# One decode step of attention and MLP: w2's first half loaded ahead of V, masked exponentials, and wo's rows 0 to 15 in one load

## The chip, the cores and the metric

The kernel runs on one core of a Trainium2 chip. The metric is the device time of one execution in microseconds (us), taken as the median of several runs. Beside the timed runs there is one profiled execution, whose records carry times from the start of its span. The engines are PE (matrix multiply, with PEld for its weight loads), DVE (vector), ACT (activations), POOL and SP; SP only issues loads here. Sixteen DMA engines move the data.

## The reference

One token x (1024 values) goes through an outer layernorm, then through attention and an MLP side by side, and everything is added to x:

```python
xn = _layernorm(x, axis=-1)
return x + _A_ref(xn, A_k_cache, A_v_cache, A_wq, A_wo) + _B_ref(xn, B_w1, B_b1, B_w2, B_b2)

# _A_ref: 32 query heads, 4 key/value heads, head size 128, the last W = 4096 positions of the caches
q = (x @ wq).reshape(B, Sq, Hq, Dh).transpose(0, 2, 1, 3)
k = jnp.repeat(k_cache[:, :, Sk - W:, :], rep, axis=1)   # rep = 8 query heads share one k/v head
v = jnp.repeat(v_cache[:, :, Sk - W:, :], rep, axis=1)
p = _softmax(jnp.einsum("bhqd,bhkd->bhqk", q, k) * (Dh ** -0.5))
o = jnp.einsum("bhqk,bhkd->bhqd", p, v)
return o.transpose(0, 2, 1, 3).reshape(B, Sq, Hq * Dh) @ wo

# _B_ref: y = _layernorm(x); h = gelu(y @ w1 + b1), 3584 values; return h @ w2 + b2
```

All weights are bf16: wq is 1024 x 4096, wo 4096 x 1024, w1 1024 x 3584, w2 3584 x 1024. With one token, every weight is used once, so the kernel has to bring some 40 MB on the chip for very little arithmetic.

## The kernel before

The program is a list of steps, each with its engine, the names that it reads and the names that it writes. `Plan` turns these names into semaphore waits; on each engine the steps run in the order in which they are written. All large loads are issued by SP, in one queue, in this order: a first row of wq (8 KB for each of the 128 partitions), K (4 MB), the rest of wq in loads of one, two and four rows, b1 and b2, w1 in two halves, V (4 MB), w2's rows 0 to 5, 6 to 13 and 14 to 27, wo's rows 0 to 7 and 8 to 15, and wo's rows 16 to 31 cut at 8, 12, 14 and 15. "Row" here means one row of the `(p c) n` view: row c of w2 is 1024 values for each of the 128 partitions.

Four buffers of 32 KB for each partition, `slot[0]` to `slot[3]`, hold all of this in turn, so a load also waits until the buffer's last reader is done. Slot 0 holds K, then w1's second half, then wo's rows 0 to 15. Slot 1 holds wq's first half, w1's first half and w2's rows 14 to 27. Slot 2 holds wq's second half, V, and wo's rows 16 to 31. Slot 3 holds K transposed in blocks (`kt_scr`), then w2's rows 0 to 13.

The work is in these stages:

- x is spread over the partitions by four small matmuls (`x_ps`, `spread`), normalised on DVE, and laid into `xw`.
- K is transposed in 32 x 32 blocks by DVE (L341) and regrouped into `kT` by ACT (L346) and DVE (L350), while PE multiplies xw by wq (L376, in a loop).
- Scores: q is transposed and laid into `qm`, a 128 x 32 weight block for each key/value head with only that head's eight columns filled; 32 matmuls of 512 columns give the scores in `sc_ps`. Their maximum goes over the partitions through PE, and ACT takes the exponential (L457) into `e128`, with the sums in `l_loc`.
- w1: eight rows, each in four column tiles of PE, in two parts, `w1_part(0)` before and `w1_part(1)` behind the maximum. DVE adds b1 (`h_pre`, L471), ACT takes gelu, DVE transposes it into `hT` and copies it into `hTf`.
- V: the exponentials are transposed in blocks into `eTb` (L461), and 32 matmuls of 512 columns (`v_step`, L502) multiply blocks of 128 columns of eTb by one position of all four heads. Each partition holds 32 positions of each head. The 32 rows of the result hold every query head against every key/value head; `gmask`, scaled by the reciprocal of the sums (`grs`), picks each head's own on DVE (`o_m`, `o_f`, `o_bf`).
- w2: DVE multiplies 21 of its 28 rows by hTf and adds them up in two accumulators, `run[0]` and `run[1]` (L489): nine rows before it looks at V's result, twelve behind. PE does the other seven, `PE_ROWS`.
- wo: o is spread over the partitions (`o8`), and PE multiplies its 32 rows. Rows 0 to 15 go one at a time, 16 to 23 in pairs on two column tiles, all into `sc_ps`; DVE adds these to run[0] (L557), the result is added by PE to rows 24 to 31 (`acc_a`, `acc_b`), DVE and ACT cast it, and two small loads store it.

Of the kernel before, what the change touches and what calls it, by code (L numbers as in the profile page):

```python
# [142 lines left out]
def kernel(  # L143
# [27 lines left out]
    NJQ = NQ // 512  # L171
    WQ4 = W // 4
# [21 lines left out]
    misc = ps("misc", [P, 512])  # L194
    qo_ps = ps("qo_ps", [P, 512])
# [20 lines left out]
    def op(eng, fn, r=(), w=()):  # L216
        plan.add(eng, fn, r, w)

    def dma(eng, out_ap, in_ap, r=(), w=(), over=()):
        q = plan.engines[eng]  # L220
        plan.add(eng, lambda: q.dma_start(out=out_ap, in_=in_ap), r, w, True, over)  # L221
# [18 lines left out]
    def mm32(out_ap, w_ap, x_ap, start, stop, r, w, pos=None):  # L240
        op("pe", lambda: pe.matmul(out_ap, lhsT=w_ap, rhs=x_ap, start=start, stop=stop, tile_position=pos), r, w)  # L241
# [10 lines left out]
    for i, a, b in wq_cuts:  # L252
# [6 lines left out]

    spread = sb("spread", [Hq, 4, P], BF16)  # L260
# [20 lines left out]

    x_ps, tot = misc[:, 0:C], misc[:, 16:17]
# [4 lines left out]
    op("dve", lambda: dve.tensor_copy(out=xf, in_=x_ps), ("misc",), ("xf",))  # L287
# [32 lines left out]
    op("dve", lambda: dve.tensor_reduce(out=sel4, in_=ident_f.rearrange("p (r h) -> p h r", r=4), axis=AX.X, op=ALU.add), ("ident_f",), ("sel4",))  # L320
    qm = sb("qm", [P, Hkv, Hq], BF16)
# [11 lines left out]
                                          compare_op=ALU.is_equal, fill=0.0, base=0, pattern=[[-1, Hq], [0, Hq]], channel_multiplier=1), ("xb32",), ("run0",))  # L333

# [45 lines left out]
    qz, zrow = qm.rearrange("p g h -> p (g h)")[0:Hq, :], spread.rearrange("p u n -> p (u n)")  # L380
# [40 lines left out]
    qm_d = qm.rearrange("p g h -> p (g h)")  # L421
    qm_d = bass.AP(tensor=qm_d.tensor, offset=qm_d.offset, ap=[list(qm_d.ap[0]), [Hq + REP, Hkv], [1, REP]])
    op("dve", lambda: dve.tensor_copy(out=qm_d, in_=qT_ps.rearrange("p k g -> p g k")), ("qo",), ("qm",))  # L423
    for g in range(Hkv):
        for R in range(4):
            ldw(qm[:, g, :], (0, 32 * R), ("qm",))
        for a in range(2):
            for R in range(4):
                kv = kT[:, R, :, :].rearrange("p u (b r h) -> p h b u r", r=8, h=Hkv)[:, g, 16 * a:16 * a + 16]
                mm(sc_ps[32 * R:32 * R + 32, a, :].rearrange("p (b r u) -> p b u r", r=8, u=4), qm[:, g, :], kv,  # L430
                   g == 0, g == Hkv - 1, (0, 32 * R), kt_keys, (f"sc{a}",))
# [4 lines left out]
    w2_t = [slot[i][:, :14 * D].rearrange("p (r n) -> p r n", r=14) for i in (3, 1)]  # L436
    for a, b in ((0, 6), (6, 14)):
        dma("sp", w2_t[0][:, a:b, :], w2_v[:, a:b, :], (), (f"w20{a}",), kt_srcs)
# [6 lines left out]
    m_row = sb("m_row", [1, Hq], FP32)  # L445
    op("dve", lambda: dve.tensor_reduce(out=m_row, in_=mT_ps.rearrange("a (r h) -> a h r", r=4), axis=AX.X, op=ALU.max), ("misc",), ("m_row",))
    m_rep = sb("m_rep", [1, 4, Hq], FP32)
    op("dve", lambda: dve.tensor_copy(out=m_rep, in_=m_row.unsqueeze(1).to_broadcast([1, 4, Hq])), ("m_row",), ("m_rep",))
    mc_ps = misc[:, 128:129]
    mm32(mc_ps, m_rep.rearrange("a r h -> a (r h)"), ones_f[0:1, 0:1], True, True, ("m_rep", "ones_f"), ("misc",))  # L450
# [8 lines left out]
    eTb = sb("eTb", [P, WQ4 + 96], BF16)  # L459
    op("pool", lambda: pool.memset(eTb[:, WQ4:], 0.0), (), ("eTb_pad",))  # L460
    op("dve", lambda: dve.transpose(out=eTb[:, :WQ4], in_=e128), ("e128",), ("eTb",))  # L461
# [4 lines left out]
    grs = sb("grs", [Hq, Hkv], FP32)  # L466
    op("dve", lambda: dve.tensor_scalar_mul(out=grs, in0=gmask, scalar1=rs), ("gmask", "rs"), ("grs",))


    h_pre = sb("h_pre", [P, 2, NH], FP32)  # L470
    op("dve", lambda: dve.tensor_tensor(out=h_pre, in0=acc2[:, :, :NH], in1=b1x.rearrange("p (b n) -> p b n", b=2), op=ALU.add), ("acc2", "b1x"), ("h_pre",))  # L471
    h_sb = sb("h_sb", [P, 2 * NH], BF16)
    op("act", lambda: act.activation(out=h_sb, in_=h_pre.rearrange("p b n -> p (b n)"), func=ACT.Gelu_apprx_tanh), ("h_pre",), ("h_sb",))
    hT = sb("hT", [P, CW2, 32], BF16)
# [18 lines left out]
    for c in dve_rows[:9]:  # L493
        running(c)


    o_all = qo_ps[0:Hq, :]
    v_in = ("eTb", "eTb_pad", "v0", "slot2")

    def v_step(c, first, last):  # L500
        cols = eTb[:, bass.ds(32 * c, P)] if not isinstance(c, int) else eTb[:, 32 * c:32 * c + P]
        return pe.matmul(qo_ps, lhsT=cols, rhs=v4[:, :, c, :], start=first, stop=last)  # L502
# [14 lines left out]
    o_m = sb("o_m", [Hq, Hkv, Dh], FP32)  # L517
    op("dve", lambda: dve.tensor_tensor(out=o_m, in0=o_all.rearrange("h (g d) -> h g d", g=Hkv), in1=grs.unsqueeze(2).to_broadcast([Hq, Hkv, Dh]), op=ALU.mult), ("qo", "grs"), ("o_m",))
    o_f = sb("o_f", [Hq, Dh], FP32)
    op("dve", lambda: dve.tensor_reduce(out=o_f, in_=o_m.rearrange("h g d -> h d g"), axis=AX.X, op=ALU.add), ("o_m",), ("o_f",))  # L520
    o_bf = sb("o_bf", [Hq, Dh], BF16)
    op("dve", lambda: dve.tensor_copy(out=o_bf, in_=o_f), ("o_f",), ("o_bf",))
    for c in dve_rows[9:]:
        running(c)
# [15 lines left out]
    hcol = lambda c: hT[:, c, 0:1]  # L540
    o8_ps = misc[:, 160:192]
# [71 lines left out]
```

## Time and profile before

| what | us |
|---|---|
| median of 3 timed runs (lowest, highest) | 99.94 (99.74, 100.01) |
| profiled execution | 99.68 |
| its span | 98.4 |
| DMA: share of 16 engines, bytes | 95.7%, 39.86 MB |
| DVE busy | 73.1 |
| PE busy | 56.0 |
| ACT busy | 30.8 |
| POOL busy | 9.9 |

A line of the timeline has the start, the length, the engine and line, what is written and read, the shape, how many instructions were merged, and, in brackets, the idle time before it and what ended that. A line of the chain of waits in order of time has the start, the length and what the time was spent on. The line of a DMA queue has packets, MB and the time its packets took as a share of 16 engines.

### The profile page before, as it was taken

How to read it: one execution, taken by the hardware profiler on the slowest of the kernel's cores; microseconds unless marked ns; L12 is line 12 of the kernel's file. 1: busy time of each engine (PE TensorE's matmuls, PEld its weight loads, DVE VectorE, ACT ScalarE, POOL GpSimd, SP SyncE). 2: the span in 40 equal slices, each digit the busy share in tenths (PEclk: the TensorE clock that was granted, in tenths of full speed). 3: DMA queues.
4: the chain of work that ended last, by engine and by line, in shares of the span. 5: the costliest groups of instructions: out<-in, count | busy, mean ns of one | idle time of the engine just before them, and what ended most of it. 6: DMA issues, size and time to landing. Idle time of an engine off the chain costs nothing.

```text
span 98.4 us, 951 instructions
## 1 busy us (share of the span) xinstructions
PE 56.0 (57%) x323; PEld 16.0 (16%) x220; DVE 73.1 (74%) x75; ACT 30.8 (31%) x29; POOL 9.9 (10%) x22
## 2 busy tenths in 40 slices
PE   0140400699200699930899547977771839595792
PEld 0040000133000234300212211211210101111130
DVE  0146407999999999999005595999989999999231
ACT  0600000099999899992002193000000000000001
POOL 0626810000000670000000000000000000000000
PEclk9999999999996559999579998599999999999999
DMA  3999979999999899989799999999898999999980
GB/s 60 487 426 453 440 310 470 433 533 426 440 426 403 373 385 513 408 373 513 330 426 426 423 438 430 425 426 480 385 524 343 433 426 433 426 433 406 396 323 1
DMA packets 3084, 39.86 MB, mean 405 GB/s; under 512 B 390, under 2 KB 396, under 8 KB 780
## 3 DMA queue, kind: packets, MB, share of 16 engines
q1 hardware_dynamic: 3034, 39.86, 95.7%
q10 hardware_dynamic: 50, 0.00, 0.0%
HBM read 39.86 MB, written 0.00 MB: 405 GB/s over the span
## 4 chain that ended last, share of the span: by engine, by line
DMA 67%; PE 22%; issue 4%; SPq 2%; DVE 0%
DMA slot<-in_A_wq_dram 29%; DMA slot<-in_A_wo_dram 21%; DMA slot<-in_A_v_cache_dram 17%; PE qo_ps L502 12%; PE acc L376 9%; SPq L221 2%; PE acc L241 1%; DVE res L576 0%; PE acc L235 0%
## 5 line engine op out<-in xcount | busy, mean ns | idle before, releaser
L346 ACT COPY kT<-slot 32x1024 bf16<-32x1024 bf16 (+1 forms) x18 | 23.9, 1327 | 15.9 <-DVE slot L341 15.7
L489 DVE SCALAR_TENSOR_TENSOR run<-slot,hTf,run 128x1024 f32<-128x1024 bf16 x20 | 24.2, 1272 | 0.1
L376 PE MATMUL acc<-slot,xw 128*128 x48 | 15.4, 495 | 13.7 <-DMA slot<-in_A_wq_dram 13.7
L341 DVE STREAM_TRANSPOSE slot<-slot 128x4096 bf16<-128x4096 bf16 x4 | 17.4, 4414 | 3.6 <-DMA slot<-in_A_k_cache_dram 3.6
L502 PE MATMUL qo_ps<-slot,eTb 128*128 (+1 forms) x32 | 11.6, 437 | 4.3 <-issue 2.6
L350 DVE COPY kT<-slot 32x4096 bf16<-32x4096 bf16 x10 | 13.2, 1320 | 0.2
L235 PE MATMUL sc_ps<-slot,o 128*1 128x512 bf16 x48 | 9.1, 378 | 4.3 <-DMA slot<-in_A_wo_dram 4.3
L376 PEld LDWEIGHTS acc<-slot,xw 128*128 x48 | 5.5, 115 | 24.3 <-issue 21.9
L577 ACT CAST res<-acc 33x224 bf16<-33x224 f32 x1 | 0.3, 339 | 20.5 <-PE acc L235 20.5
L235 PE MATMUL sc_ps<-kT,qm 128*32 128x512 bf16 x32 | 5.3, 853 | 0.3 <-DVE qm L423 0.3
L502 PEld LDWEIGHTS qo_ps<-slot,eTb 128*128 (+1 forms) x32 | 3.1, 97 | 12.5 <-issue 9.8
L545 ACT CAST o<-misc 128x32 bf16<-128x32 f32 x1 | 0.2, 186 | 15.0 <-PE misc L241 15.0
L227 PEld LDWEIGHTS <-o 128*1 128x1 bf16 x40 | 2.4, 83 | 13.9 <-issue 13.3
L435 DVE COPY sc<-sc_ps 128x512 f32<-128x512 f32 x1 | 0.7, 691 | 4.9 <-PE sc_ps L235 4.9
L241 PE MATMUL acc<-spread,qm 32*128 32x512 bf16 x4 | 1.6, 498 | 3.7 <-POOL qm L322 3.7
L235 PE MATMUL sc_ps<-slot,hT 128*1 128x512 bf16 x14 | 3.2, 378 | 0.5 <-DMA slot<-in_B_w_dram 0.5
L235 PE MATMUL acc<-slot,yT 128*1 128x448 bf16 x64 | 3.4, 353 | 0.0
L434 ACT COPY sc<-sc_ps 128x512 f32<-128x512 f32 x1 | 0.6, 585 | 8.0 <-PE sc_ps L235 8.0
L241 PE MATMUL qo_ps<-selq,q_sb 128*128 128x4 bf16 x8 | 0.4, 166 | 4.3 <-DVE q_sb L395 4.3
L241 PE MATMUL misc<-x,spread 32*128 32x8 bf16 x4 | 0.3, 168 | 4.4 <-POOL spread L262 4.4
L557 DVE TENSOR_TENSOR run<-sc_ps,run 33x512 f32<-33x512 f32 x2 | 1.3, 678 | 1.8 <-PE sc_ps L235 1.8
L235 PE MATMUL acc<-slot,o 128*1 128x288 bf16 (+1 forms) x32 | 2.2, 272 | 0.7 <-DMA slot<-in_A_wo_dram 0.6
(88 smaller groups left out, 43.6 us busy)
## 6 DMA issues: line engine op xcount, KB each, us to landing
slot<-in_B_w_dram SPq DMA_DIRECT2D x3, 3584.0 KB, 16.7
slot<-in_A_wo_dram SPq DMA_DIRECT2D x3, 2048.0 KB, 23.7
slot<-in_A_k_cache_dram SPq DMA_DIRECT2D x1, 4096.0 KB, 14.0
slot<-in_A_wq_dram SPq DMA_DIRECT2D x1, 4096.0 KB, 28.6
slot<-in_A_v_cache_dram SPq DMA_DIRECT2D x1, 4096.0 KB, 16.8
slot<-in_A_wq_dram SPq DMA_DIRECT2D x2, 1024.0 KB, 9.8
slot<-in_A_wq_dram SPq DMA_DIRECT2D x1, 2048.0 KB, 19.3
slot<-in_B_w_dram SPq DMA_DIRECT2D x1, 2048.0 KB, 21.5
```

The source lines that it names most:

```text
L221: plan.add(eng, lambda: q.dma_start(out=out_ap, in_=in_ap), r, w, True, over)
L227: return pe.add_instruction(mybir.InstLdweights(name=nc.get_next_instruction_name(), engine=i.engine, tile_size=(P, 32), tile_position=pos ...
L235: return pe.add_instruction(mybir.InstMatmult(name=nc.get_next_instruction_name(), engine=i.engine, start_tensor_calc=start, stop_tensor_c ...
L241: op("pe", lambda: pe.matmul(out_ap, lhsT=w_ap, rhs=x_ap, start=start, stop=stop, tile_position=pos), r, w)
L341: op("dve", lambda s=s: dve.transpose(out=scr[:, s, :], in_=k2[:, s, :]), ("k", "slot0"), (f"scr{s}",))
L346: op("act", lambda s0=s0, s1=s1, R=R, Cd=Cd: act.copy(out=kT[32 * Cd:32 * Cd + 32, R, s0:s1, :].rearrange("p s (c j) -> p (s c) j", j=32), ...
L350: op("dve", lambda R=R, Cd=Cd: dve.tensor_copy(out=kT[32 * Cd:32 * Cd + 32, R, :, :].rearrange("p s (c j) -> p (s c) j", j=32), in_=T3[32 ...
L376: pe.matmul(acc2[:, b, :], lhsT=xw[:, bass.ds(32 * n + 512 * i, P)], rhs=slot[1 + i][:, bass.ds(1024 * n + 512 * b, 512)], start=False, st ...
L435: op("dve", lambda: dve.tensor_copy(out=sc[:, 0:512], in_=sc_ps[:, 0, :]), ("sc0",), ("scs0",))
L489: op("dve", lambda: dve.scalar_tensor_tensor(out=t, in0=wap, scalar=hTf[:, c:c + 1], in1=t, op0=ALU.mult, op1=ALU.add), (key, "hTf", f"run ...
L502: return pe.matmul(qo_ps, lhsT=cols, rhs=v4[:, :, c, :], start=first, stop=last)
L557: op("dve", lambda half=half: dve.tensor_tensor(out=run[0][0:33, 512 * half:512 * half + 512], in0=bulk[:, half, :], in1=run[0][0:33, 512 ...
```

## The change

V is loaded in K's form. Partition p = 4r + g now holds 128 positions in a row of head g, 32 KB in one piece, where it held 32 positions of all four heads in four pieces of 8 KB. The x path, `sel4`, `qm` and the score matmuls are laid out anew: the four column tiles of the scores are now the four heads. For V, the transposed exponentials are put in V's order of partitions by two matmuls with a permutation (`perm`, `e_ps`), and ACT writes them four times, each time multiplied by a column of `own` that is 1 on one head's partitions and 0 elsewhere (`own_heads`). The result, `eM`, has 32 columns for each position, so that each matmul of V takes four positions at once; the four useful blocks of its result are copied out by DVE (`o_u`) and added.

The loads change buffers and order: w2's rows 0 to 13 go to slot 2, in one load ahead of V, and V goes to slot 3. wo's rows 0 to 15 come in one load instead of two, and wo's rows 16 to 31 wait for the DVE rows 0 to 13 of w2. DVE does sixteen w2 rows before it looks at V's result and five behind, PE does its w2 rows ahead of spreading o, and wo's rows 0 to 15 go in pairs too.

```diff
+    e_ps = ps("e_ps", [P, NCH * 4, REP])
...
+    fours = sb("fours", [Hq, P], BF16)
+    op("pool", lambda: pool.memset(fours, 1.0), (), ("fours",))
...
-    for u in range(4):
-        mm32(x_ps, spread[:, u, :], x32[:, 8 * u:8 * u + 8], u == 0, u == 3, ("spread", "x32"), ("misc",))
+    op("dve", lambda: dve.tensor_reduce(out=own, in_=ident_f.rearrange("p (r g) -> p g r", g=Hkv), axis=AX.X, op=ALU.add), ("ident_f",), ("own",))
+    mm32(x_ps, fours, x32, True, True, ("fours", "x32"), ("misc",))
...
+    op("pool", lambda: pool.tensor_copy(out=perm.rearrange("p (r g) -> p r g", g=Hkv), in_=ident_f.rearrange("p (g r) -> p r g", g=Hkv)), ("ident_f", "run0"), ("perm",))
...
-    v_sb = slot[2]
-    v4 = v_sb.rearrange("p (g c d) -> p g c d", g=Hkv, c=NCH)
-    dma("sp", v_sb.rearrange("p (g n) -> p g n", g=Hkv), A_v_cache[0, :, Sk - W:Sk, :].rearrange("g (p c) d -> p g (c d)", p=P), (), ("v0",), ("slot2",))
+    w2_t = [slot[i][:, :14 * D].rearrange("p (r n) -> p r n", r=14) for i in (2, 1)]
+    dma("sp", w2_t[0], w2_v[:, 0:14, :], (), ("w20",), ("slot2",))
+    v_sb = slot[3]
...
-                mm(sc_ps[32 * R:32 * R + 32, a, :].rearrange("p (b r u) -> p b u r", r=8, u=4), qm[:, g, :], kv,
-                   g == 0, g == Hkv - 1, (0, 32 * R), kt_keys, (f"sc{a}",))
+                mm(sc_ps[32 * g:32 * g + 32, a, :].rearrange("p (w q r) -> p w q r", q=4, r=8), qm[:, g, u, :], kv,
+                   u == 0, u == 3, (0, 32 * g), kt_keys, (f"sc{a}",))
...
-    for a, b in ((0, 6), (6, 14)):
-        dma("sp", w2_t[0][:, a:b, :], w2_v[:, a:b, :], (), (f"w20{a}",), kt_srcs)
+    dma("sp", v_sb, A_v_cache[0, :, Sk - W:Sk, :].rearrange("g (r c) d -> r g (c d)", r=P // Hkv), (), ("v0",), kt_srcs)
...
+    for b in range(2):
+        mm32(e_ps[:, 64 * b:64 * b + 64, :], perm, eTb[:, 64 * b:64 * b + 64, :], True, True, ("perm", "eTb"), (f"e_ps{b}",))
...
+    def own_heads(g):
+        op("act", lambda: act.activation(out=eM[:, :, REP * g:REP * g + REP], in_=e_ps, func=ACT.Copy, scale=own[:, g:g + 1]),
+           ("e_ps0", "e_ps1", "own"), (f"eM{g}",))
...
-    for c in dve_rows[:9]:
+    for c in dve_rows[:16]:
         running(c)
...
-    for a in (0, 8):
-        dma("sp", wo_t[0][:, a:a + 8, :], wo_v[:, a:a + 8, :], (), (f"wo0{a}",), ("slot0",))
+    dma("sp", wo_t[0], wo_v[:, 0:16, :], (), ("wo0",), ("slot0",))
...
-        dma("sp", wo_t[1][:, a:b, :], wo_v[:, 16 + a:16 + b, :], (), (f"wo1{a}",), ("slot2",))
+        dma("sp", wo_t[1][:, a:b, :], wo_v[:, 16 + a:16 + b, :], (), (f"wo1{a}",), ("w20",))
+    for u in range(4):
+        op("dve", lambda u=u: dve.tensor_copy(out=o_u[:, u, :], in_=qo_ps[32 * u:32 * u + 32, Dh * u:Dh * u + Dh]), ("qo",), (f"o_u{u}",))
...
+    bulk_rows(PE_ROWS, w2_row, hcol, "hT", first=True)
...
-    bulk_rows(list(range(16)), wo_row, ocol, "o8")
-    bulk_rows(list(range(16, NB)), wo_row, ocol, "o8", last=True, groups=2)
+    bulk_rows(list(range(NB)), wo_row, ocol, "o8", last=True, groups=2)
```

More of the change, by code (lines that the diff above doesn't have):

```diff
@@ L258 @@
     op("act", lambda: act.activation(out=dummy[:, 0:1], in_=mhalf[0:1, 0:1], func=ACT.Exp), ("mhalf",), ("act_warm",))
+    fours = sb("fours", [Hq, P], BF16)
+    op("pool", lambda: pool.memset(fours, 1.0), (), ("fours",))
+    op("pool", lambda: pool.affine_select(out=fours, in_=fours, compare_op=ALU.is_ge, fill=0.0, base=0,
+                                          pattern=[[1, P]], channel_multiplier=-4), ("fours",), ("fours",))
+    op("pool", lambda: pool.affine_select(out=fours, in_=fours, compare_op=ALU.is_ge, fill=0.0, base=3,
+                                          pattern=[[-1, P]], channel_multiplier=4), ("fours",), ("fours",))
+    ident_f = sb("ident_f", [P, P], FP32)
+    op("pool", lambda: pool.memset(ident_f, 0.0), (), ("ident_f",))
+    op("pool", lambda: pool.affine_select(out=ident_f, in_=ident_f, compare_op=ALU.not_equal, fill=1.0, base=0,
+                                          pattern=[[-1, P]], channel_multiplier=1), ("ident_f",), ("ident_f",))
     spread = sb("spread", [Hq, 4, P], BF16)
@@ L319 @@
     sel4 = sb("sel4", [P, Hq], FP32)
-    op("dve", lambda: dve.tensor_reduce(out=sel4, in_=ident_f.rearrange("p (r h) -> p h r", r=4), axis=AX.X, op=ALU.add), ("ident_f",), ("sel4",))
-    qm = sb("qm", [P, Hkv, Hq], BF16)
+    op("dve", lambda: dve.tensor_reduce(out=sel4.rearrange("p (g h) -> p g h", g=Hkv), in_=ident_f.rearrange("p (g u h) -> p g h u", g=Hkv, u=4),
+                                        axis=AX.X, op=ALU.add), ("ident_f",), ("sel4",))
+    qm = sb("qm", [P, Hkv, 4, Hq], BF16)
     op("pool", lambda: pool.memset(qm, 0.0), (), ("qm",))
@@ L378, in wq_rows @@
         return rows
-    qz, zrow = qm.rearrange("p g h -> p (g h)")[0:Hq, :], spread.rearrange("p u n -> p (u n)")
+    qz, zrow = qm[0:Hq, 0, :, :].rearrange("p u h -> p (u h)"), spread.rearrange("p u n -> p (u n)")
     for b in range(2):
@@ L420 @@
             mm32(qT_ps[:, k, :], blk, selq, True, True, (f"q_sb{b}", "selq"), ("qo",))
[L421 to L426, printed above, removed]
+    qm_d = bass.AP(tensor=qm.tensor, offset=qm.offset, ap=[list(qm.ap[0]), [4 * Hq, Hkv], [Hq + REP, 4], [1, REP]])
+    op("dve", lambda: dve.tensor_copy(out=qm_d, in_=qT_ps.rearrange("p k g -> p g k").unsqueeze(2).to_broadcast([P, Hkv, 4, REP])), ("qo",), ("qm",))
+    for u in range(4):
+        for g in range(Hkv):
+            ldw(qm[:, g, u, :], (0, 32 * g), ("qm",))
         for a in range(2):
-            for R in range(4):
-                kv = kT[:, R, :, :].rearrange("p u (b r h) -> p h b u r", r=8, h=Hkv)[:, g, 16 * a:16 * a + 16]
-                mm(sc_ps[32 * R:32 * R + 32, a, :].rearrange("p (b r u) -> p b u r", r=8, u=4), qm[:, g, :], kv,
-                   g == 0, g == Hkv - 1, (0, 32 * R), kt_keys, (f"sc{a}",))
+            for g in range(Hkv):
+                kv = kT.rearrange("p q s (w u r k) -> p k u (s w) q r", u=4, r=8, k=Hkv)[:, g, u, 16 * a:16 * a + 16, :, :]
+                mm(sc_ps[32 * g:32 * g + 32, a, :].rearrange("p (w q r) -> p w q r", q=4, r=8), qm[:, g, u, :], kv,
+                   u == 0, u == 3, (0, 32 * g), kt_keys, (f"sc{a}",))
     w1_part(0)
@@ L458 @@
     op("act", lambda: act.activation(out=dummy[:, 1:2], in_=mhalf[0:1, 0:1], func=ACT.Gelu_apprx_tanh), ("mhalf",), ("act_warm",))
-    eTb = sb("eTb", [P, WQ4 + 96], BF16)
-    op("pool", lambda: pool.memset(eTb[:, WQ4:], 0.0), (), ("eTb_pad",))
-    op("dve", lambda: dve.transpose(out=eTb[:, :WQ4], in_=e128), ("e128",), ("eTb",))
+    eTb = sb("eTb", [P, NCH * 4, REP], BF16)
+    op("dve", lambda: dve.transpose(out=eTb.rearrange("p c h -> p (c h)"), in_=e128), ("e128",), ("eTb",))
+    for b in range(2):
+        mm32(e_ps[:, 64 * b:64 * b + 64, :], perm, eTb[:, 64 * b:64 * b + 64, :], True, True, ("perm", "eTb"), (f"e_ps{b}",))
     rs_ps = misc[0:Hq, 144:145]
@@ L465 @@
     op("dve", lambda: dve.reciprocal(out=rs, in_=rs_ps), ("misc",), ("rs",))
-    grs = sb("grs", [Hq, Hkv], FP32)
-    op("dve", lambda: dve.tensor_scalar_mul(out=grs, in0=gmask, scalar1=rs), ("gmask", "rs"), ("grs",))
+    eM = sb("eM", [P, NCH * 4, Hq], BF16)
+    def own_heads(g):
+        op("act", lambda: act.activation(out=eM[:, :, REP * g:REP * g + REP], in_=e_ps, func=ACT.Copy, scale=own[:, g:g + 1]),
+           ("e_ps0", "e_ps1", "own"), (f"eM{g}",))
     h_pre = sb("h_pre", [P, 2, NH], FP32)
     op("dve", lambda: dve.tensor_tensor(out=h_pre, in0=acc2[:, :, :NH], in1=b1x.rearrange("p (b n) -> p b n", b=2), op=ALU.add), ("acc2", "b1x"), ("h_pre",))
+    own_heads(0)
     h_sb = sb("h_sb", [P, 2 * NH], BF16)
     op("act", lambda: act.activation(out=h_sb, in_=h_pre.rearrange("p b n -> p (b n)"), func=ACT.Gelu_apprx_tanh), ("h_pre",), ("h_sb",))
+    for g in (1, 2, 3):
+        own_heads(g)
     hT = sb("hT", [P, CW2, 32], BF16)
@@ L492, with v_step @@
     dve_rows = [c for c in range(CW2) if c not in PE_ROWS]
-    for c in dve_rows[:9]:
+    for c in dve_rows[:16]:
         running(c)
[L497 to L502, printed above, removed]
+    v_in = ("eM0", "eM1", "eM2", "eM3", "v0", "slot3")
+    eM_w = eM.rearrange("p c h -> p (c h)")
+    def v_step(w, first, last):
+        if isinstance(w, int):
+            cols, keys = eM_w[:, P * w:P * w + P], v_sb[:, 512 * w:512 * w + 512]
+        else:
+            cols, keys = eM_w[:, bass.ds(P * w, P)], v_sb[:, bass.ds(512 * w, 512)]
+        return pe.matmul(qo_ps, lhsT=cols, rhs=keys, start=first, stop=last)
     def v_rows(i):
@@ L511 @@
     wo_t = [slot[s].rearrange("p (r n) -> p r n", r=16) for s in (0, 2)]
-    for a in (0, 8):
-        dma("sp", wo_t[0][:, a:a + 8, :], wo_v[:, a:a + 8, :], (), (f"wo0{a}",), ("slot0",))
+    dma("sp", wo_t[0], wo_v[:, 0:16, :], (), ("wo0",), ("slot0",))
     cuts = [0, 8, 12, 14, 15, 16]
     for a, b in zip(cuts[:-1], cuts[1:]):
-        dma("sp", wo_t[1][:, a:b, :], wo_v[:, 16 + a:16 + b, :], (), (f"wo1{a}",), ("slot2",))
-    o_m = sb("o_m", [Hq, Hkv, Dh], FP32)
-    op("dve", lambda: dve.tensor_tensor(out=o_m, in0=o_all.rearrange("h (g d) -> h g d", g=Hkv), in1=grs.unsqueeze(2).to_broadcast([Hq, Hkv, Dh]), op=ALU.mult), ("qo", "grs"), ("o_m",))
+        dma("sp", wo_t[1][:, a:b, :], wo_v[:, 16 + a:16 + b, :], (), (f"wo1{a}",), ("w20",))
+    o_u = sb("o_u", [Hq, 4, Dh], FP32)
+    for u in range(4):
+        op("dve", lambda u=u: dve.tensor_copy(out=o_u[:, u, :], in_=qo_ps[32 * u:32 * u + 32, Dh * u:Dh * u + Dh]), ("qo",), (f"o_u{u}",))
     o_f = sb("o_f", [Hq, Dh], FP32)
-    op("dve", lambda: dve.tensor_reduce(out=o_f, in_=o_m.rearrange("h g d -> h d g"), axis=AX.X, op=ALU.add), ("o_m",), ("o_f",))
+    op("dve", lambda: dve.tensor_reduce(out=o_f, in_=o_u.rearrange("h u d -> h d u"), axis=AX.X, op=ALU.add), ("o_u0", "o_u1", "o_u2", "o_u3"), ("o_f",))
     o_bf = sb("o_bf", [Hq, Dh], BF16)
-    op("dve", lambda: dve.tensor_copy(out=o_bf, in_=o_f), ("o_f",), ("o_bf",))
-    for c in dve_rows[9:]:
+    op("act", lambda: act.activation(out=o_bf, in_=o_f, func=ACT.Copy, scale=rs), ("o_f", "rs"), ("o_bf",))
+    for c in dve_rows[16:]:
         running(c)
```

35 lines of the change are left out of this document (14 added, 21 removed).

## The prediction

> **What bounds the kernel now.** I read the page's slices and queues first, then its chain, then the DMA packets stretch by stretch, and last the order of time at the end.
>
> ```profile
> PE 56.0 (57%) x323; PEld 16.0 (16%) x220; DVE 73.1 (74%) x75; ACT 30.8 (31%) x29; POOL 9.9 (10%) x22
> ...
> DMA  3999979999999899989799999999898999999980
> ...
> q1 hardware_dynamic: 3034, 39.86, 95.7%
> ```
>
> No engine is full, but one queue is: 39.86 MB keep the 16 DMA engines busy for 95.7% of the span, from the second slice to the last but one. The chain in order of time shows only parts of that:
>
> ```profile
> 42.60 16.78 DMA slot<-in_A_v_cache_dram
> ...
> 73.69 0.33 SPq L221
> ...
> 75.49 20.74 DMA slot<-in_A_wo_dram
> ```
>
> It says that V landed at 59.37, that PE read V until 73.69, and that only then the second half of wo was issued. That looks like a wait worth removing, but the last wo load took 20.74 us because w2 and the first half of wo stood ahead of it in the queue. A later or earlier issue changes nothing while the queue holds work. What counts is how long the packets take. The DMA view of a window gives packets, MB and the share of 16 engines, so share x 16 x window / packets is the time of one packet. For the windows 51 to 57 (V), 24 to 30 (wq, last load), 60 to 62 (w2, first load) and 81.6 to 84.6 (wo):
>
> ```profile
> q1 hardware_dynamic: 311, 2.55, 100.8%
> ```
> ```profile
> q1 hardware_dynamic: 80, 2.62, 101.1%
> ```
> ```profile
> q1 hardware_dynamic: 70, 0.86, 101.8%
> ```
> ```profile
> q1 hardware_dynamic: 80, 1.31, 102.5%
> ```
>
> So 8 KB take 0.311 us, 32 KB 1.213, 12 KB 0.465, 16 KB 0.615; the window 68 to 74 (96 packets, 2.75 MB, 106.6%) gives 1.066 for 28 KB. These lie on a line: bytes at about 27.2 GB/s per engine plus about 9 ns per packet. Last, the end:
>
> ```profile
> 81.40 3.61 PE L235 MATMUL sc_ps<-slot,o 128*1 128x512 bf16 x16 [1.71 <-DMA slot<-in_A_wo_dram]
> 86.29 3.61 PE L235 MATMUL sc_ps<-slot,o 128*1 128x512 bf16 x16 [1.28 <-DMA slot<-in_A_wo_dram]
> 91.18 1.89 PE L235 MATMUL sc_ps<-slot,o 128*1 128x512 bf16 x16 [1.28 <-DMA slot<-in_A_wo_dram]
> 93.67 1.03 PE L235 MATMUL acc<-slot,o 128*1 128x288 bf16 x16 [0.60 <-DMA slot<-in_A_wo_dram]
> ```
> ```profile
> 90.05 1.23 DVE L525 TENSOR_TENSOR run<-run 128x1024 f32<-128x1024 f32 x1
> 93.11 1.28 DVE L557 TENSOR_TENSOR run<-sc_ps,run 33x512 f32<-33x512 f32 x2 [1.83 <-PE sc_ps L235]
> ```
>
> PE waits for every piece of wo, so the loads set the end. DVE finishes its own sums at 91.28 and waits 1.83 us for PE: that slack is the only cover on DVE, and the change spends part of it.
>
> **The change part by part.** The sum is made against the profiled execution, 99.68 us (span 98.4 plus 1.28 around it); the median of the three timed runs, 99.94, is 0.26 above it.
>
> *Loads.* The bytes are the same. V goes from 512 rows of 8 KB to 128 of 32 KB: per engine 32 x 0.311 = 9.96 us become 8 x 1.213 = 9.70, so -0.26. w2's rows 0 to 13 go from 12 and 16 KB to 28 KB: 8 x (0.465 + 0.615) = 8.64 become 8 x 1.066 = 8.53, -0.11. wo's rows 0 to 15 go from 16 KB twice to 32 KB: 16 x 0.615 = 9.84 become 9.70, -0.14. Together -0.51. But the landings of wo's pieces above are 4.89 us apart for 8 packets per engine, 0.611 each, so packets overlap by some 4 ns; with that taken off each packet the three terms are -0.16, -0.08 and -0.11, together -0.35. The other end is 0 (the engines' rate, not the packets, sets it). I take -0.40, nearer to the landings.
>
> The order of the loads counts as well: V now stands behind w2's first half, which takes 8.5 us. w2 is issued where V was (42.60, when PE is done with wq), V where w2 was (46.09, when the last copy out of slot 3 ends), and both moments lie ahead of the queue, which holds w1 until 48 to 49. wo's second half waits on DVE's row 13 of w2 instead of PE's last V step: 80.4 instead of 73.69 (below), with five issues of 0.43 us each on SP, nothing but the output behind them. wo's first half keeps the queue busy until about 85, so 4 us of cover remain; without it each us late would be a us at the end.
>
> [...]
>
> *Start.* The x path swaps four matmuls and a copy for two masks on POOL, one matmul, a reduction of ident_f (own; like sel4's, 0.73), a multiply and a reduction (0.16 each): xf at about 5.6 instead of 4.84. POOL clears four times as much of qm (0.20 to at most 0.8) before b1x, whose load SP issues some 1.3 us later at most, behind loads already queued. xw would be ready near 10.1; PE's first use is 18.11, after a DMA wait, and DVE's next work is K at 15.28 against 11.7 plus 0.8. Cost 0; the cover is 3 us on DVE and 8 on PE. spread and selq move behind the new masks and are first used later still. POOL's new perm copy at 35 replaces the clearing of eTb's pad (1.24). One of DVE's ten copies took 2.19 instead of 1.22 while POOL worked there, so this can shift DVE by -0.97 to +0.97; I take 0, as one POOL step replaces another.
>
> *Scores.* The same 16 weight loads and 32 matmuls of 512 columns, with the same step of four elements in the reads but whole-row writes. Bounds: 3.3 us faster (at w1's rate, 64 in 3.4 us) to 1.5 slower (8 rounds of 0.853 instead of 5.29); I take 0, the row of the same shape. The copy into qm writes 128 instead of 32 columns: +0.10 (0.191 at 32, 0.692 at 512 columns).
>
> *After the exponentials.* PE now waits for eTb (58.80, with the 0.10 above 58.90), does two perm matmuls (0.05 to start, 0.38, the second 0.21 later), then the row sums (0.22): 59.77 instead of 57.79. The reciprocal waits behind that in DVE's order, and h_pre behind it: it starts at 59.93 instead of 59.01 (grs, 0.22, is gone). So gelu, hT, hTf and all rows come 0.92 later: row 0 at 64.05. On ACT the four masked copies of 1024 columns cost 1.02 each (0.585 at 512 and 0.339 at 288 columns from PSUM; at most 1.15, the exponential's); the first ends at 60.6, before h_pre at 61.0, the other three by 65.1. That is before V, so hidden.
>
> *V and the rows.* V lands at 59.37 + 8.50 - 0.16 = 67.7. Its 32 steps take 14.2 us as before (59.51 to 73.69, one loop round per 0.92 at a granted clock of 0.50 and of 1.00 alike): 82.05. DVE does rows 0 to 15 first: 1.87 for two and 14 x 1.207 = 16.9, until 82.8; so it does not wait for V. Rows 14 and 15 need w2's second half, which lands near 76.3. Then four copies from PSUM (0.29 each at 128 columns; 0.17 to 0.35 as bounds) and the reduction (1.00) end at 85.0, against 1.9 for o_m, o_f and o_bf before: +0.3. The other five rows (6.0) and the sum of the accumulators (1.23) end at 92.25 instead of 91.28. PE's wo rows 16 to 23 will be summed by 93.07 - 0.40 = 92.67, so DVE has 0.4 us left and costs 0.
>
> *PE's end.* Its w2 rows (3.18) fit between 82.05 and o_bf; ACT's o_bf and o8 and the spread give o8 at 85.9, when wo's first half lands (86.25 - 0.3). Rows 0 to 15 now go in pairs, 0.43 a pair: 3.6 us, until 89.6, against a landing at 90.8. Cost 0, cover 1.2 us. The tail after the last landing is unchanged.
>
> Sum: -0.40 + 0 = 99.28 in the profiled execution, 99.54 as a median: 99.5.
>
> **The rivals.**
> 1. DVE becomes the bound (slower). Its place is L537, the sum of the accumulators; the point is 92.67, and every us beyond it is a us at the end, since the sums (1.28) and the matmuls that add them follow without a gap. My chain ends at 92.25; 0.42 later removes the cover, 0.82 eats the gain, 1.12 is 0.3 slower than before. For it: POOL's collision (0.97), a slower score stage (up to 1.5), four copies from PSUM at their upper bound (0.24). Against it: each of them alone stays near the cover, and none has a row that makes it likelier than its opposite. Time 99.9 where it only eats the gain; with the collision and half the score bound 99.94 - 0.40 + (1.72 - 0.42) = 100.8.
> 2. No gain from packet size: the engines move 39.86 MB at one rate. For it: from w1 to V's landing 11.5 MB took 27.0 us (427 GB/s), and the next 7.34 MB, w2 in packets of 12 to 28 KB, 430. Time 99.9.
> 3. V's rows collide in memory: adjacent partitions of one load now lie 16 MB apart. K is loaded in just this form, and its window 6 to 13 gives 94 packets at 101.9%, 1.214 us each, as wq's. If the four heads' rows took turns instead, V would take 4 x 9.7: +29 us, 129. [...]
> 4. One load of wo is late: rows 0 to 7 cannot start at 81.4. With V's steps 1.2 us later than forecast, the pairs end after 90.8 and push the sums; at +2 us that is 100.3.
> 5. Scores run faster and nothing changes, as DMA is the bound; but with more gained between loads than packets show, 99.2.
>
> **How the numbers follow.** 0.3% is about what a measurement of this kernel can tell from no change: faster is below 99.64, slower above 100.24. The forecast has 0.50, of which 0.06 ends within 0.3%; rival 1 0.26 (0.12 same, 0.14 slower); rival 2 0.10 (same); rival 3 0.02 and rival 4 0.06 (slower); rival 5 0.06 (faster). So faster 0.50, same 0.28, slower 0.22. The likeliest one's own range is 99.35 to 99.75. The range reaches over rivals 2 and 5 and most of 1 and 4: 99.2 to 100.5.
>
> **What would show it.** V's packets at 32 KB and 1.21 us, wo's first half landing near 86.0, the last load near 95.8; w2's first row on DVE near 64.05, L537 ending near 92.3 and the sums of L567 still waiting for PE. Wrong if the sums wait for DVE instead, if a DMA slice before the end is empty, or if the last load lands no earlier than 96.2.

## The result, and the profile after

The changed kernel takes 99.43 us (median of 11 runs, 99.31 to 100.25) against 99.87 (median of 11 runs of the kernel before, 99.74 to 100.45): a ratio of 0.9963 with a 95% interval of 0.9946 to 0.9979. The profiled execution took 99.38 us, its span 98.1. The forecast was 99.5 as a median, 0.996 of the 99.94 known then, and 99.28 for the profiled execution.

The page of the changed kernel first: its DVE and DMA slices, and the DMA queue with packets, MB and share.

```profile
DVE  0255647999999999999206665999999997999431
...
DMA  3899989999999989989988999998899999999980
...
q1 hardware_dynamic: 2362, 39.86, 95.6%
```

The bytes are the same, the queue is as full as before (95.6% against 95.7%), but it holds 2362 packets instead of 3034. For V, the DMA view of the window 59 to 66 has:

```profile
q1 hardware_dynamic: 94, 3.08, 102.1%
```

That is 1.021 x 16 x 7 / 94 = 1.217 us for 32 KB, as K and wq had it. The end in order of time, PE and then DVE (start, length, line, what, and the idle time before it):

```profile
81.92 3.18 PE L236 MATMUL sc_ps<-slot,hT 128*1 128x512 bf16 x14
85.03 0.26 PE L242 MATMUL misc<-o_bf,spread 32*128 32x32 bf16 x4
86.00 3.62 PE L236 MATMUL sc_ps<-slot,o 128*1 128x512 bf16 x32 [0.71 <-DMA slot<-in_A_wo_dram]
90.91 1.89 PE L236 MATMUL sc_ps<-slot,o 128*1 128x512 bf16 x16 [1.28 <-DMA slot<-in_A_wo_dram]
93.39 1.03 PE L236 MATMUL acc<-slot,o 128*1 128x288 bf16 x16 [0.60 <-DMA slot<-in_A_wo_dram]
```
```profile
90.27 1.23 DVE L537 TENSOR_TENSOR run<-run 128x1024 f32<-128x1024 f32 x1
92.83 1.28 DVE L567 TENSOR_TENSOR run<-sc_ps,run 33x512 f32<-33x512 f32 x2 [1.34 <-PE sc_ps L236]
```

PE still waits for every piece of wo, and each piece comes 0.27 to 0.29 us earlier (86.00 for 86.29, 90.91 for 91.18, 93.39 for 93.67). DVE still waits for PE at the sums, 1.34 us where it was 1.83. The score stage, which was expected unchanged, is shorter; before and after (the first line is from the kernel before):

```profile
47.48 5.29 PE L235 MATMUL sc_ps<-kT,qm 128*32 128x512 bf16 x32 [0.29 <-DVE qm L423]
```
```profile
47.78 3.94 PE L236 MATMUL sc_ps<-kT,qm 128*32 128x512 bf16 x32 [0.39 <-DVE qm L428]
```

One view now misleads. The page's chain of the changed kernel, the work that ended last followed back from the end, begins

```profile
DVE 55%; DMA 29%; PE 9%; ACT 3%; issue 2%; SPq 1%; DVEq 0%
```

and in order of time it runs from DVE's rows to the issue of wo's second half:

```profile
77.72 1.29 DVE run L498
...
79.03 0.33 SPq L222
...
79.40 13.95 DMA slot<-in_A_wo_dram
```

It goes back through the last issue, not through the queue in front of it. Read alone it names DVE as the bound. Run e6 shows that it is not.

### The profile page after: what moved, and what is told of

It is laid out like the page before. It is cut to its first block, busy times and chain, and to the rows that moved or that the text cites. A ratio compares the mean times of both kernels' runs of the same rounds, so it can differ in the third digit from the quotient of the medians.

```text
span 98.1 us, 955 instructions
## 1 busy us (share of the span) xinstructions
PE 51.1 (52%) x321; PEld 15.3 (16%) x219; DVE 75.3 (77%) x78; ACT 35.3 (36%) x34; POOL 10.6 (11%) x22
## 2 busy tenths in 40 slices
DMA packets 2412, 39.86 MB, mean 406 GB/s; under 512 B 358, under 2 KB 364, under 8 KB 748
## 3 DMA queue, kind: packets, MB, share of 16 engines
q1 hardware_dynamic: 2362, 39.86, 95.6%
HBM read 39.86 MB, written 0.00 MB: 406 GB/s over the span
## 4 chain that ended last, share of the span: by engine, by line
DVE 55%; DMA 29%; PE 9%; ACT 3%; issue 2%; SPq 1%; DVEq 0%
DVE slot L348 18%; DVE run L498 15%; DMA slot<-in_A_k_cache_dram 14%; DMA slot<-in_A_wo_dram 14%; DVE kT L357 14%; PE sc_ps L236 4%; PE acc L236 2%; DVE hT L484 2%; DVE eTb L463 1%; ACT e L460 1%; DVE m_loc L445 1%; DVE h_pre L477 1%; ACT h_sb L480 1%; PE acc L242 1%; DVE q_sb L402 1%
## 5 line engine op out<-in xcount | busy, mean ns | idle before, releaser
L514 PE MATMUL qo_ps<-slot,eM 128*128 (+1 forms) x32 | 11.3, 443 | 12.2 <-DMA slot<-in_A_v_cache_dram 9.3
L236 PE MATMUL sc_ps<-slot,o 128*1 128x512 bf16 x48 | 5.5, 378 | 2.0 <-DMA slot<-in_A_wo_dram 2.0
L514 PEld LDWEIGHTS qo_ps<-slot,eM 128*128 (+1 forms) x32 | 3.1, 98 | 20.1 <-issue 18.0
L473 ACT ACTIVATE eM<-e_ps,own 128x1024 bf16<-128x1024 f32 x4 | 4.2, 1107 | 0.5 <-PE e_ps L242 0.5
L236 PE MATMUL sc_ps<-kT,qm 128*32 128x512 bf16 x32 | 3.9, 647 | 0.4 <-DVE qm L428 0.4
L228 PEld LDWEIGHTS <-o 128*1 128x1 bf16 x40 | 1.7, 83 | 8.1 <-issue 7.1
L321 DVE TENSOR_SCALAR yT<-xn,st 128x8 bf16<-128x8 f32 x1 | 2.1, 2135 | 0.7 <-POOL st L319 0.7
```

Source lines behind the costliest of these rows:

```text
L228: return pe.add_instruction(mybir.InstLdweights(name=nc.get_next_instruction_name(), engine=i.engine, tile_size=(P, 32), tile_position=pos ...
L236: return pe.add_instruction(mybir.InstMatmult(name=nc.get_next_instruction_name(), engine=i.engine, start_tensor_calc=start, stop_tensor_c ...
L321: op("dve", lambda: dve.tensor_scalar(out=yT, in0=xn, scalar1=st12[:, 2:3], scalar2=st12[:, 6:7], op0=ALU.subtract, op1=ALU.mult), ("xn", ...
L473: op("act", lambda: act.activation(out=eM[:, :, REP * g:REP * g + REP], in_=e_ps, func=ACT.Copy, scale=own[:, g:g + 1]), ("e_ps0", "e_ps1" ...
L514: return pe.matmul(qo_ps, lhsT=cols, rhs=keys, start=first, stop=last)
```

## The experiments

Two theories were set against each other. The packet theory: the DMA queue sets the end, and its time is a sum over packets, bytes plus a small fixed cost for each. The rate theory: 39.86 MB take their time whatever the pieces, and the gain came from elsewhere, the order of the loads for one. Beside them stood DVE as the bound and PE late with wo. Many of the times scatter by a few tenths of a us, so the small terms are read from the traces as well, as the time from the landing of wq's last load to that of wo's row 24, both seen as PE's first matmul on them. The edits below leave out lines that only rename the keys by which steps wait for loads.

| kernel | wq's last | wo row 24 | between |
|---|---|---|---|
| before | 32.78 | 93.67 | 60.89 |
| before, wo in one load and pairs (e10) | 33.85 | 94.74 | 60.89 |
| changed | 32.91 | 93.39 | 60.48 |
| changed again (e1) | 32.85 | 93.60 | 60.75 |
| changed, wo in two loads (e2) | 32.92 | 93.54 | 60.62 |
| changed, other order of score writes (e5) | 32.88 | 93.40 | 60.52 |
| changed, one more DVE step (e6) | 32.81 | 93.33 | 60.52 |
| changed, two more (e7) | 34.08 | 94.58 | 60.50 |
| changed, V in four loads (e12) | 32.70 | 93.88 | 61.18 |
| changed, w2 and wo's first half in 2 KB packets (e3) | 32.80 | 96.69 | 63.89 |

The five kernels whose loads are those of the changed kernel lie at 60.48 to 60.75, four of them at 60.48 to 60.52; the kernel before at 60.89, twice. So the loads gained about 0.37 to 0.41 us by the four that agree and 0.14 by e1: one trace can be off by 0.25. (In e8, e9 and e11 PE comes too late to its rows of wo to show their landing; e4 changes the first loads.)

**e1: the changed kernel again.**

> The changed kernel once more, as the yardstick for the runs beside it. Packet theory (fewer, longer packets shorten the one full queue): a ratio of 0.996 to the kernel before, the last wo load landing near 95.9. Rate theory (the engines move 39.86 MB at one rate whatever the pieces, and the gain came from somewhere else): the same ratio, so this run alone tells nothing apart.

99.54 us (median of 12), against 99.83 beside it for the kernel before; ratio 0.9945 (0.9905 to 0.9986). The gain is there again.

**e2: wo's rows 0 to 15 in two loads again.**

```diff
-    dma("sp", wo_t[0], wo_v[:, 0:16, :], (), ("wo0",), ("slot0",))
+    for a in (0, 8):
+        dma("sp", wo_t[0][:, a:a + 8, :], wo_v[:, a:a + 8, :], (), (f"wo0{a}",), ("slot0",))
```

> The changed kernel with wo's rows 0 to 15 in two loads of 16 KB rows again, still in pairs on PE. Packet theory: 16 packets of 0.611 to 0.615 us for each engine instead of 8 of 1.213, so 0.1 to 0.14 us longer than the changed kernel beside it (ratio to the kernel before about 0.997). Rate theory: no difference (below 0.05 us). [...]

99.54 us, the median of e1 beside it, ratio 0.9965 (0.9929 to 1.0002). In the trace 60.62 lies 0.1 above the four equal ones, but below e1. That agrees with 0.1 us and can't show it. The prediction put no price on a load as such, and one load more, issued by SP behind the other, shows none beyond the 0.10 to 0.14 us by which e2 lies above the four.

**e3: w2 and wo's first half in packets of 2 KB.**

```diff
-    dma("sp", w2_t[0], w2_v[:, 0:14, :], (), ("w20",), ("slot2",))
+    for h in range(2):
+        dma("sp", w2_t[0][:, h:14:2, :], w2_v[:, h:14:2, :], (), (f"w20{h}",), ("slot2",))
```

and the same for w2's second half and wo's rows 0 to 15.

> The changed kernel with w2's two halves and wo's rows 0 to 15 loaded as even rows and odd rows, two loads each: the same bytes to the same places, in packets of 2 KB. Packet theory: the small packets at the end of the kernel before take 0.084 to 0.087 us each, so w2 takes 2 x 112 x 0.084 = 18.8 us instead of 17.1 and wo's half 128 x 0.084 = 10.8 instead of 9.7: 2.8 us longer than the changed kernel (ratio to the kernel before about 1.024). Rate theory: no difference beyond 0.3 us.

102.97 us, 3.4 above e1; ratio 1.029 (1.023 to 1.035); 63.89 between the landings, 3.4 above 60.5. The DMA view of the window 72 to 76:

```profile
DMA packets 772, 1.55 MB, mean 387 GB/s; under 512 B 16, under 2 KB 16, under 8 KB 772
...
q1 hardware_dynamic: 772, 1.55, 105.2%
```

So a packet of 2 KB takes 1.052 x 64 / 772 = 0.087 us. The queue is just as full and moves 387 GB/s; V's window above has 440 (3.08 MB in 7 us). This is the run that decides between the theories: the same bytes to the same places, in smaller pieces, cost 3.4 us (2.8 expected, from 0.084 a packet). The edit also makes three loads more, but e2 shows no cost of one more load beyond about 0.1 us. The rate theory falls for pieces of 2 KB; for the pieces of 8 to 32 KB of this change there are the table and e12.

**e4: K first, and wq's rows 0 to 3 in one load.**

```diff
-wq_cuts = ((0, 1, 2), (0, 2, 4), (1, 0, 4))
+wq_cuts = ((1, 0, 4),)
```

with K issued first and `wq_v[:, 0:4, :]` as one load behind it.

> The changed kernel with K first in the queue and wq's rows 0 to 3 in one load of 32 KB rows behind it, instead of one, one and two rows around K. Packet theory: 8 x (0.311 + 0.311 + 0.615) = 9.90 us become 9.70, so 0.1 to 0.2 us shorter than the changed kernel (ratio to the kernel before about 0.9945). K lands 2.4 us earlier, so DVE's chain ends up to 2.4 us earlier, which should change nothing as the loads set the end. A rival: wq's first half now lands at about 22 and PE is done with it at about 29.5 instead of 25.3, and w1's first half waits for that; if the queue runs dry, at about 31.4, the loss is what is missing there.

100.43 us, ratio 1.0047 (1.0013 to 1.0081): 0.9 slower than e1 where 0.1 to 0.2 faster was expected. K landed 2.0 us earlier (DVE's transposes start at 13.34 instead of 15.38), but wq's last load at 33.18 instead of 32.91, and V at 68.71 instead of 67.88. w1's first half was issued at 30.47 instead of 25.57, since PE was done with wq's first half only then. That is the rival named beforehand, but the windows around 31 show no empty stretch in the queue: from 30 to 58 its share is 1.00, as in the changed kernel. Of the loss 0.27 us stand by wq's last load and 0.56 more come between it and V; behind V both kernels take the same (25.53 and 25.51 us to wo's row 24). What holds up the loads there stays open. As a step beyond the change it failed.

**e5: the order of the score writes.**

```diff
-                mm(sc_ps[32 * g:32 * g + 32, a, :].rearrange("p (w q r) -> p w q r", q=4, r=8), ...
+                mm(sc_ps[32 * g:32 * g + 32, a, :].rearrange("p (w r q) -> p w q r", q=4, r=8), ...
```

> The changed kernel with only the order changed in which the 32 score matmuls write their 512 columns: innermost a step of four, as in the kernel before, instead of whole rows. The reads stay as they are. The scores then stand at permuted positions, so V is weighted wrongly; the work is the same. The score stage took 5.29 us before and 3.94 after. If the writes made the difference: 5.3 us, DVE's rows 1.35 us later, the 1.34 us that DVE waits for PE at the sums used up, and the time within 0.1 us of the changed kernel. If the reads made it: 3.9 us and no other difference.

99.57 us, ratio 0.9978 (0.9949 to 1.0007). The score stage takes 6.22 us instead of 3.94 (5.3 was expected), and DVE has no idle time left before the sums:

```profile
47.77 6.22 PE L236 MATMUL sc_ps<-kT,qm 128*32 128x512 bf16 x32 [0.39 <-DVE qm L428]
```
```profile
91.82 1.23 DVE L537 TENSOR_TENSOR run<-run 128x1024 f32<-128x1024 f32 x1
93.15 1.28 DVE L567 TENSOR_TENSOR run<-sc_ps,run 33x512 f32<-33x512 f32 x2
```

So the writes made the stage shorter, not the reads. The 5.29 us of the kernel before are not a fixed figure, though. Its unchanged stage took 5.34 us in e11, 5.74 in e10 and 6.23 in e9:

```profile
48.47 6.23 PE L235 MATMUL sc_ps<-kT,qm 128*32 128x512 bf16 x32 [0.29 <-DVE qm L423]
```

It is longer the longer the granted clock stays at 0.50 in it: 3.2 us of the stage in the kernel before and e11, 4.1 in e10, 5.2 in e9 and 5.1 in e5. With whole rows the stage took 3.8 to 4.0 us in every run, in the changed kernel with the clock at 0.50 for 3.3 of its 3.94 us. So the step in the writes alone accounts for e5, and what whole rows save goes with the clock: 1.35 us in this pair, 2.3 between e5 and the changed kernel.

DVE's rows come 2.3 us later in e5 (64.99 instead of 62.70), and the median is 0.17 above that of e6, measured beside it, because nearly all of it is covered.

**e6 and e7: one and two more DVE steps behind o_f.**

```diff
+    junk = slot[1][:, 14336:15360]
+    for _ in range(1):      # e7: range(2)
+        op("dve", lambda: dve.tensor_tensor(out=junk, in0=run[1], in1=run[1], op=ALU.add), ("run1",), ("junk",))
     for c in dve_rows[16:]:
```

> The changed kernel with one more DVE step of 128 x 1024 (about 1.2 us, its result unused) behind o_f. DVE waits 1.34 us for PE at the sums, so if the loads set the end and DVE has that slack: no difference (ratio to the kernel before 0.996). If DVE set the end: 1.2 us longer (1.008).

> The same with two such DVE steps, 2.4 us. Slack of 1.34: 1.1 us longer than the changed kernel (ratio to the kernel before 1.007), with the sums waiting for nothing. If the loads hid all DVE work: no difference. If DVE set the end already: 2.4 us longer (1.020).

One step: 99.40 us, ratio 0.9946 (0.9914 to 0.9978), no difference. Two steps: 100.27, ratio 1.0042 (1.0028 to 1.0057), 0.87 above e6 (1.1 expected). In e6 the sums start at 92.76, a moment after L540 (there the sum of the accumulators) ended at 92.62; in e7 right behind it:

```profile
91.39 1.23 DVE L540 TENSOR_TENSOR run<-run 128x1024 f32<-128x1024 f32 x1
92.76 1.28 DVE L570 TENSOR_TENSOR run<-sc_ps,run 33x512 f32<-33x512 f32 x2
```
```profile
93.85 1.23 DVE L540 TENSOR_TENSOR run<-run 128x1024 f32<-128x1024 f32 x1
95.18 1.28 DVE L570 TENSOR_TENSOR run<-sc_ps,run 33x512 f32<-33x512 f32 x2
```

(The profiled execution of e7 started its loads 1.2 us later than the others; its times are read against each other, or from the landing of wq's last load.) So DVE had 1.2 to 1.3 us to spare, and beyond them it costs. Counted from wq's last load the sums come 1.15 us later in e7 than in e6, DVE's last cast only 0.85: the tail behind the sums gives 0.3 back, which is why the time shows 0.87 and not 1.1. The chain's "DVE 55%" was no bound.

**e8: wo's rows 0 to 15 one at a time.**

```diff
-    bulk_rows(list(range(NB)), wo_row, ocol, "o8", last=True, groups=2)
+    bulk_rows(list(range(16)), wo_row, ocol, "o8")
+    bulk_rows(list(range(16, NB)), wo_row, ocol, "o8", last=True, groups=2)
```

> The changed kernel with wo's rows 0 to 15 one at a time on PE again, as in the kernel before, instead of in pairs. wo's half lands at 86.0 in one piece, and the 32 matmuls then take 7.2 us (2 x 3.61) instead of 3.62: rows 0 to 15 end at 93.2, 2.3 us behind the landing of the next piece (90.9). Everything behind follows: 2.3 us longer less what the last rows catch up, so 1.8 to 2.3 us (ratio to the kernel before 1.015 to 1.019). Rival: PE catches up while it waits for the later pieces and nothing is seen.

101.29 us, ratio 1.018 (1.013 to 1.024), 1.9 above e6:

```profile
86.05 8.15 PE L236 MATMUL sc_ps<-slot,o 128*1 128x512 bf16 x45 [0.69 <-DMA slot<-in_A_wo_dram]
```

PE is busy from 86.05 to 94.2 without a pause and never catches up. The single load of wo is only free together with the pairs.

**e9, e10, e11: parts of the change in the kernel before.** Beside them the kernel before took 100.73 (median of 13, 99.88 to 101.64).

```diff
 # e9, e10
-    for a in (0, 8):
-        dma("sp", wo_t[0][:, a:a + 8, :], wo_v[:, a:a + 8, :], (), (f"wo0{a}",), ("slot0",))
+    dma("sp", wo_t[0], wo_v[:, 0:16, :], (), ("wo0",), ("slot0",))
 # e10 also
-    bulk_rows(list(range(16)), wo_row, ocol, "o8")
-    bulk_rows(list(range(16, NB)), wo_row, ocol, "o8", last=True, groups=2)
+    bulk_rows(list(range(NB)), wo_row, ocol, "o8", last=True, groups=2)
 # e11 alone
-    for a, b in ((0, 6), (6, 14)):
-        dma("sp", w2_t[0][:, a:b, :], w2_v[:, a:b, :], (), (f"w20{a}",), kt_srcs)
+    dma("sp", w2_t[0], w2_v[:, 0:14, :], (), ("w20",), kt_srcs)
```

> The kernel before with only wo's rows 0 to 15 in one load instead of two, PE taking them one at a time as it did. Packet theory alone: 0.1 us shorter. But rows 0 to 7 then start at 86.2 instead of 81.4, and 32 matmuls one at a time take 7.2 us, until 93.4, 2.2 us behind the landing of rows 16 to 23: 1.9 us longer (ratio 1.019), as in the run with rows taken singly in the changed kernel.

> The same with all 24 rows in pairs. The 16 rows end at 86.2 + 3.6 = 89.8, ahead of the next landing, so only the packets are left: 0.1 us shorter than the kernel before or, if the packets of 16 and 32 KB cost the same, no difference (ratio 0.998 to 1.001).

> The kernel before with w2's rows 0 to 13 in one load instead of two, still behind V. Packet theory alone: 0.1 us shorter. But the load lands at 67.9, and DVE starts its rows there instead of at 63.13: 4.8 us later, less the 0.25 it waited for V and the 1.83 it waited for PE at the sums: 2.7 us longer (ratio 1.027). If the loads hid DVE's work whatever its start: no difference.

e9: 104.25 us, ratio 1.039 (1.033 to 1.046), 3.5 longer where 1.9 was expected. PE waited 4.84 us for the load, from 82.33 to 87.17, and the windows that follow (length, then busy time of PE, PEld, DVE, ACT and POOL, then the granted clock of PE, the DMA share and GB/s) show what else was lost:

```profile
87.17 10.11 PE L235 MATMUL sc_ps<-slot,o 128*1 128x512 bf16 x45 [4.84 <-DMA slot<-in_A_wo_dram]
```
```profile
81.00:83.00 2.00, 1.33 (x7) 0.25 (x3) 2.00 (x2) 0.00 (x0) 0.00 (x0) 1.00 0.88 377
83.00:85.00 2.00, 0.00 (x0) 0.00 (x0) 2.00 (x3) 0.00 (x0) 0.00 (x0) 0.84 0.95 410
85.00:87.00 2.00, 0.00 (x0) 0.00 (x0) 2.00 (x3) 0.00 (x0) 0.00 (x0) 0.50 0.93 393
87.00:89.00 2.00, 1.83 (x5) 0.26 (x2) 2.00 (x2) 0.00 (x0) 0.00 (x0) 0.50 0.98 418
89.00:91.00 2.00, 2.00 (x7) 0.29 (x3) 2.00 (x3) 0.00 (x0) 0.00 (x0) 0.50 0.99 418
91.00:93.00 2.00, 2.00 (x10) 0.43 (x5) 1.76 (x2) 0.00 (x0) 0.00 (x0) 0.96 0.94 391
```

The granted clock fell to 0.50 during the wait and stayed there for about four more us of work. The same matmuls took 8.15 us in e8 at a granted clock of 1.00 and 10.11 here: 2.0 of the 3.5 us. A mean of 0.84 from 83 to 85 puts the fall near 84.4, 2.0 us into the wait; 0.96 from 91 to 93 puts the return near 91.2, after 4.0 us of work. In the changed kernel V, and with it PE's w2 rows, come later (81.92 to 85.1), so the gap before wo is 0.71 us, and the granted clock from 86 to 90 was 1.00.

e10: 100.59 us, ratio 0.997 (0.992 to 1.002), and 60.89 between the landings, as before. The granted clock fell to 0.50 here too, near 86.8, 3.2 us into a wait of 3.67 us, and the 24 rows in pairs took 6.79 us; they ended at 94.13, ahead of the next landing at 94.74, so it cost nothing. 0.1 us is too little to be seen.

e11: 103.15 us, ratio 1.031 (1.025 to 1.037), 2.4 longer by the medians:

```profile
68.01 1.28 DVE L488 SCALAR_TENSOR_TENSOR run<-slot,hTf,run 128x1024 f32<-128x1024 bf16 x1 [5.02 <-DMA slot<-in_B_w_dram]
...
95.93 1.28 DVE L556 TENSOR_TENSOR run<-sc_ps,run 33x512 f32<-33x512 f32 x2
```

DVE starts its rows at 68.01 and sums at 95.93 instead of 93.11, as worked out. w2's first half in one load needs the place ahead of V.

**e12: V in four loads.**

```diff
-    dma("sp", v_sb, A_v_cache[0, :, Sk - W:Sk, :].rearrange("g (r c) d -> r g (c d)", r=P // Hkv), (), ("v0",), kt_srcs)
+    v_rows_d = A_v_cache[0, :, Sk - W:Sk, :].rearrange("g (r c) d -> r g (c d)", r=P // Hkv)
+    for n in range(4):
+        dma("sp", v_sb[:, 4096 * n:4096 * n + 4096], v_rows_d[:, :, 4096 * n:4096 * n + 4096], (), (f"v{n}",), kt_srcs)
```

> The changed kernel with V in four loads, each 8 KB of every partition, so V comes in the packets it had in the kernel before, to the same places. Packet theory: 32 x 0.311 = 9.96 us (9.83 with the overlap of 4 ns a packet) instead of 9.70: from the landing of wq's last load to that of V it takes 0.13 to 0.26 us longer than the 34.97 to 35.05 of the changed kernel and its variants, and the end follows by as much (ratio to the kernel before 0.997 to 0.999, within the noise of the times). Rate theory: 34.97 to 35.05 again.

100.01 us, ratio 1.0005 (0.996 to 1.005). V lands 35.61 us behind wq's last load; in the changed kernel, e2 and e5 to e8 it was 34.97 to 35.10. That is 0.5 to 0.6 longer, more than the packets explain (0.13 to 0.26). But e1, with the loads of the changed kernel, had 35.23 there, so up to 0.25 of it is scatter. The kernel before took 100.07 beside it: with V in 8 KB pieces, and the new order and buffers kept, no gain is left to be seen, though the interval still reaches 0.996. That speaks against the order as the source of the gain. The sign agrees with the packets; the size of V's term, and what the four loads as such add to it, is not settled.

## Why the prediction was right

*The loads.* -0.40 was the whole of the forecast, and it is about what was found: -0.37 to -0.41 between the landings, -0.44 in the medians, -0.30 in the profiled execution (99.38 against 99.68; wq's last load landed 0.13 later in it). e3 shows the mechanism, that longer pieces shorten a full queue, with eight times the effect (3.4 us). How the 0.4 divides over V, w2 and wo was only worked out from packets; e2, e10 and e12 could not resolve it. The single terms agree less well than the total: joining wo's load was worth 0.00 in e10 (0.11 to 0.14 forecast), cutting V's cost 0.6 in e12 (0.16 to 0.26 forecast). So the closeness of the total is in part luck.

*The order of the loads.* Nothing ran dry. wo's second half was issued at 79.03 instead of the 80.4 forecast, and wo's first half landed at 86.0.

*Memory collisions* (rival 3) did not come: V's packets take 1.217 us with the four heads 16 MB apart, as K's did (1.214).

*The start* cost nothing: xf was done at 5.37, near the 5.6 forecast, and K set DVE's next step at 15.38. Of the cover on DVE 1.96 us were left, where about 2.8 were forecast. POOL's perm copy took 1.27, the clearing it replaced 1.24, and one of DVE's copies took 2.19 again. Zero was the right choice between -0.97 and +0.97.

*The scores* are the step that failed, without harm. The prediction took 0 between -3.3 and +1.5 because the row had the same shape; it was -1.35, and e5 shows that the writes, whole rows instead of a step of four, made it. DVE's first row started at 62.70 instead of 64.05. That this is 1.35 too is luck: the scores began 0.20 later than forecast (47.78 instead of 47.58), and the stretch behind them was 0.20 shorter. The slack at the sums was 1.34 where 0.4 was forecast. With scores of 5.29 us the rows would have come 1.35 later, the wait of 0.64 for V would have taken up part of it, and by this estimate 0.63 of slack would have been left, near the forecast; in e5, at 6.22, none is left.

*Behind that* the terms held: the masked copies took 1.11 and 1.04 (1.02 forecast, from 0.585 at 512 columns and 0.339 at 224, not 288), V landed at 67.9 (67.7), its steps ended at 82.0 (82.05), the four copies took 1.18 (1.16), the reduction 1.02 (1.00). Since DVE was early, it now waited 0.64 us for V, which cost nothing. o8 was ready at 85.5 (85.9), and the pairs took 3.62 us (3.6).

*DVE as the bound* (rival 1) had the right place: e7 crosses the point and pays. The price was a little high: 1.1 us beyond the cover cost 0.87, not 1.1. *One load of wo being late* (rival 4) was shut out by the pairs, which e8 shows. What the prediction had not priced is the clock: with the pairs (e10) or without (e9), PE worked at a granted clock of 0.50 behind the wait for the one long load; only the pairs had room for it.

## What to carry to other kernels

Where one queue is full from end to end, count its packets and price them from the trace: the same bytes in longer rows are the gain (440 GB/s in packets of 32 KB here, 387 in packets of 2 KB); one load more or less showed nothing above 0.1 us (e2, e10). Joining loads makes the first row wait for the last one (in e10 PE's first row of wo started 4.87 us later, counted from wq's last load), so ask first which engine starts on the early rows, and give it other work or a faster pass: here, without the place ahead of V for w2 (e11) or the pairs for wo (e8, e9), the joined loads cost 1.9 to 3.5 us, while all the longer pieces together gain a few tenths. The chain that ended last goes through the last issue, even when a full queue made that issue harmless; add work to the engine it names before believing it.

## What the runs showed of the hardware

The granted clock fell to 0.50 about 2.0 us into a wait of 4.84 us and stayed there for some 4 us of matmuls (e9); in e10 it fell 3.2 us into a wait; in the changed kernel, where PE paused for 0.71 us before the same rows, it was 1.00. Thirty-two score matmuls with four column tiles at once took 3.8 to 4.0 us when they wrote whole rows to PSUM, and 5.29 to 6.23 when the innermost step was four values, the longer the more of the stage ran at a granted clock of 0.50 (3.2 of the 5.29 us in the kernel before, 5.1 of the 6.22 in e5). A packet of 2 KB took 0.087 us (e3), one of 32 KB 1.217: 387 GB/s against 440 in a queue just as full. The same 28 and 32 KB loads, executed again, can take 0.25 us longer (e1, up to the landing of V), which is as much as the largest single term of this change.
